# Chunked attention with routed MLP: 8-token load rows, PE transposes of halves, block-diagonal V, mask as bias, scatter-add output

## Chip, cores and metric

One core of one Trainium2 chip runs one launch. The metric is the device time of that launch in microseconds. The core has a matrix engine (TensorE, PE; its weight loads are listed apart as PEld), three elementwise engines (VectorE, DVE; ScalarE, ACT; GpSimd, POOL) and a queue engine (SyncE, SP). DMAs are issued here from the SP and POOL queues and run on 16 DMA engines. Every engine works through its own instructions in order.

## The reference

Attention runs in chunks of 32 queries; each chunk sees 8 memory slots and a window of keys from 16 before it to 8 after it. Then, for each of the 4 batch entries, the 128 of 768 tokens with the highest gate score get an MLP's output, times a sigmoid of the score, added.

```
q, k, v: (4, 8, 768, 64); mem_k, mem_v: (4, 8, 8, 64)
for each chunk c of 32:                       # 24 chunks
    k_full = concat(mem_k, k[c*32-16 : c*32+40]);  v_full the same   # clipped at the ends
    a = softmax(0.125 * q_c @ k_full.T);  out_c = a @ v_full
x = out as (4, 768, 512)
for b in range(4):
    s = x[b] @ w_gate;  top = the 128 largest of s
    y = relu(x[b, top] @ w1) @ w2             # 512 -> 1024 -> 512
    out[b, top] = x[b, top] + sigmoid(s[top]) * y
```

## The kernel before

A *group* is 96 queries (three chunks) of one head with 128 key rows: 8 memory slots and a window of 120 tokens. There are 8 groups to a head, 8 heads and 4 batches. The loop runs eight *phases* of (batch, half of the heads): four heads each.

- Set-up (lines 66 to 140). `identity` and the iotas come from POOL. The mask is three extra contraction rows in `qT` and `kT` (rows 64 to 66), filled by small DMAs from SP (L116, L125, L128), and zero blocks go into `v_sh` (L139, L140).
- A phase first issues its loads (L142): per head, q and k as fp32 from SP with 768 pieces of 256 bytes each (L148), V from POOL with a cast to fp16 (L164), and a POOL copy of the memory values (L166).
- Per head (L169): PE transposes of 128x128 fp32 (L175, L181), ACT copies qT out (L177, L178), DVE copies kT out twice and then lays the windows out (L183 to L192), and POOL adds the memory keys (L193).
- Per group (L196): four score matmuls (L200), one exponential of 384 columns on ACT (L203), four value matmuls with a ones column for the sum (L206), reciprocal and scaling on DVE (L209, L210) into `x_norm`, which stays in SBUF.
- The routed MLP of a batch: scores on DVE (L234), a row of scores by DMA and a POOL broadcast (L237, L239), rank by sign sums on ACT (L253), selection matrices on DVE (L257, L265), gather matmuls (L275), two MLP layers (L288, L298), then eight update matmuls (L307) and adds on DVE (L309) into `x_norm`, and one store of the whole batch (L313). MLP `b` is hooked into later phases: scoring and rank a batch later, the rest two batches later. After the last phase the MLP of batch 2 and all of batch 3 remain.
- A scheduler sets the order on each engine from the code's order and its own estimates; at run time the orders are fixed.

## Time and profile before

| | |
|---|---|
| time, median of 3 runs | 267.44 us (265.09 to 268.04) |
| span of the profiled execution | 263.0 us |
| set-up, to the first q tile used by PE | 0 to 30.9 us |
| first value matmul | 46.6 us |
| last scaled attention tile | 197.2 us |
| remaining MLP work and stores | 197.2 to 263.0 us |
| busy share PE, DVE, ACT, POOL | 57%, 61%, 46%, 27% |

The span is one execution; the time of a run holds some microseconds around it. Busy PE time counts the modelled latency of each matmul, so it overstates how full PE is. [...]

### The profile page before, as it was taken

Reading aid. Unit: us, or ns where it says so; the run is one execution under the profiler, and the core shown is the slowest. Engines: PE = TensorE matmul, PEld = TensorE weight load, DVE = VectorE, ACT = ScalarE, POOL = GpSimd, SP = SyncE. Lnnn points to the kernel's source line nnn. Section 1 sums busy time; section 2 is a strip of 40 time slices with the busy share of each in tenths; the row PEclk is TensorE's granted clock in tenths of the full one; section 3 lists DMA queues with packets and bytes.
Section 4 is the critical chain, followed back from the end, with each engine's and each line's share of the span. In section 5 each row is a group of like instructions: output and inputs, shape, how many; then the busy total and the mean of one; then the engine's idle time right before and its main releaser. Section 6 shows DMA issues by size and latency. Waiting matters only on the chain.

```text
span 263.0 us, 3436 instructions
## 1 busy us (share of the span) xinstructions
PE 151.1 (57%) x1056; PEld 110.3 (42%) x1056; DVE 159.9 (61%) x482; ACT 120.0 (46%) x260; POOL 70.9 (27%) x117
## 2 busy tenths in 40 slices
PE   0200255878867488658847778783682575487420
...
GB/s 50 32 181 116 117 157 157 220 190 142 202 168 35 172 135 179 147 145 67 30 98 98 240 22 58 0 0 94 148 0 0 2 2 0 1 237 3 0 47 192
DMA packets 90697, 25.55 MB, mean 97 GB/s; under 512 B 85944, under 2 KB 86968, under 8 KB 90680
## 3 DMA queue, kind: packets, MB, share of 16 engines
...
## 4 chain that ended last, share of the span: by engine, by line
PE 35%; DVE 26%; ACT 11%; DMA 8%; issue 8%; SPq 6%; POOL 3%; ACTq 0%; POOLq 0%
DVE xn L309 7%; PE p_upd L307 5%; PE pst L200 5%; PE pkt L181 5%; PE p_xeT L275 4%; PE pxv L206 4%; PE pqt L175 4%; DMA ksb<-in_k_dram 4%; DMA kT<-zeros_src 4%; PE p_hT L288 4%; SPq L148 3%; PE p_ye L298 3%; ACT expS L203 2%; DVE xn L210 2%; DVE kA L183 2%
## 5 line engine op out<-in xcount | busy, mean ns | idle before, releaser
L175 PE MATMUL pqt<-identity,qsb 128*128 128x128 f32 x96 | 28.0, 414 | 30.3 <-DMA qsb<-in_q_dram 24.2
L203 ACT ACTIVATE expS<-pst 128x384 f16<-128x384 f32 x64 | 30.4, 490 | 27.2 <-PE pst L200 26.0
L200 PE MATMUL pst<-qT,kT 67*128 67x96 f16 x256 | 37.3, 268 | 8.9 <-DVE kT L191 2.4
L177 ACT CAST qT<-pqt 64x384 f16<-64x384 f32 x32 | 15.1, 471 | 52.0 <-PE pqt L175 51.6
L181 PE MATMUL pkt<-identity,ksb 128*128 128x128 f32 x96 | 27.6, 406 | 11.9 <-ACT qT L178 4.9
L164 POOL DMA_DIRECT2D vsh<-in_v_dram x30 | 28.5, 951 | 19.8 <-PE pxv L206 19.8
L206 PE MATMUL pxv<-vsh,expS 128*96 128x65 f16 x256 | 31.0, 263 | 4.9 <-DVE rd L209 2.3
L206 PEld LDWEIGHTS <-expS 128*96 128x96 f16 x256 | 28.5, 189 | 12.2 <-ACT expS L203 5.6
L175 PEld LDWEIGHTS pqt<-identity,qsb 128*128 128x128 f32 x96 | 16.0, 206 | 40.8 <-DMA qsb<-in_q_dram 19.7
L200 PEld LDWEIGHTS <-kT 67*128 67x128 f16 x256 | 25.2, 135 | 18.9 <-issue 9.7
L309 DVE TENSOR_TENSOR xn<-p_upd,xn 96x512 f32<-96x512 f32 x32 | 21.9, 683 | 18.4 <-PE p_upd L307 18.2
L183 DVE CAST kA<-pkt 64x384 f16<-64x384 f32 x32 | 17.5, 546 | 22.8 <-PE pkt L181 22.6
L253 ACT ACTIVATE junk_rk<-Bsb,scores 96x768 f32<-96x768 f32 x32 | 29.8, 932 | 0.6
L210 DVE TENSOR_TENSOR xn<-pxv,rd 96x256 f32<-96x256 f32 x64 | 26.5, 414 | 0.8
L307 PE MATMUL p_upd<-ye,selT 128*96 128x512 f16 x32 | 16.7, 522 | 16.9 <-DVE xn L309 15.1
L275 PE MATMUL p_xeT<-sel,x 96*128 96x128 f16 x128 | 18.1, 305 | 14.1 <-DVE sel L257 13.3
L166 POOL COPY vsh<-memv_all 8x512 f16<-8x512 f16 x32 | 21.7, 690 | 10.9 <-DMA memv_all<-in_mem_v_dram 10.9
L193 POOL COPY kT<-memkT_sb 64x64 f16<-64x64 f16 x32 | 6.9, 256 | 60.8 <-PE pst L200 60.8
L181 PEld LDWEIGHTS pkt<-identity,ksb 128*128 128x128 f32 x96 | 15.3, 200 | 17.0 <-ACT qT L178 7.3
L234 DVE SCALAR_TENSOR_TENSOR junk_sc<-xn,wgb 96x512 f32<-96x512 f32 x32 | 21.7, 677 | 0.2
L209 DVE RECIPROCAL rd<-pxv 96x4 f32<-96x4 f32 x64 | 11.2, 175 | 15.8 <-PE pxv L206 15.1
L275 PEld LDWEIGHTS <-x 96*128 96x128 f16 x128 | 14.3, 143 | 14.4 <-issue 13.9
...
## 6 DMA issues: line engine op xcount, KB each, us to landing
...
vsh<-in_v_dram POOLq DMA_DIRECT2D x30, 120.0 KB, 7.9
w_sb<-in_moe_w_dram POOLq DMA_DIRECT2D x2, 1024.0 KB, 11.0
...
vsh<-in_v_dram POOLq DMA_DIRECT2D x2, 105.0 KB, 4.7
qT<-ones_src SPq DMA_DIRECT2D x12, 0.5 KB
```

The source lines that it names most:

```text
L164: nc.gpsimd.dma_start(out=v_sh[8:128, h, :, 0:D], in_=_dap(v, base - 16 * D, [[D, 120], [96 * D, 8], [1, D]]))
L175: nc.tensor.transpose(out=pq[:, pr, :], in_=q_sb[:, h4, pr, :], identity=identity)
L181: nc.tensor.transpose(out=pk[:, pr, :], in_=k_sb[:, h4, pr, :], identity=identity)
L183: nc.vector.tensor_copy(out=kae[:, :, 0, :], in_=pk[0:64, :, :])
L200: nc.tensor.matmul(out=p_st[:, h4, :], lhsT=kT_ext[h4][0:67, g, :], rhs=qT_ext[h4][0:67, GQ * g:GQ * g + GQ], start=True, stop=True)
L203: nc.scalar.activation(out=es, in_=p_st[:, :, :], func=AF.Exp, bias=0.0, scale=0.125)
L206: nc.tensor.matmul(out=p_x[0:GQ, h4, :], lhsT=es[:, h4, :], rhs=v_sh[:, h4, g, :], start=True, stop=True)
L210: nc.vector.tensor_tensor(out=x_norm[0:GQ, g, :].rearrange("p (h d) -> p h d", d=D)[:, NH * hq:NH * hq + NH, :], in0=p_x[0:GQ, :, 0:D], in ...
L253: nc.scalar.activation(out=m.junk_rk[0:GQ, :], in_=m.Bsb[0:GQ, :], func=AF.Sign, bias=m.scores[0:GQ, g:g + 1], scale=-1.0, accum_out=m.cod ...
L275: nc.tensor.matmul(out=m.p_xeT[:, dch, :], lhsT=m.x16[0:GQ, g, 128 * dch:128 * dch + 128], rhs=m.sel16[0:GQ, g, :], start=(g == 0), stop=( ...
L307: nc.tensor.matmul(out=m.p_upd[0:GQ, g % 2, :], lhsT=m.selT[:, g, :], rhs=m.ye, start=True, stop=True)
L309: nc.vector.tensor_tensor(out=x[0:GQ, g, :], in0=m.p_upd[0:GQ, g % 2, :], in1=x[0:GQ, g, :], op=ALU.add)
```

## The change

Nearly the whole kernel function is rewritten.

- **Loads.** q and k are loaded by POOL with a cast to fp16, as rows of 8 tokens (512 elements, 2 KB of DRAM) on 96 partitions: 4 DMAs a batch after the first. V stays fp32 and comes from SP in rows of two tokens (512 bytes), head 0 of a pair on partitions 0 to 63 and head 1 on 64 to 127, 60 rows of window and 4 of memory.
- **Units.** The work is cut into 16 pairs of heads with 2 halves each (32 units of 4 groups). For a pair, 16 PE transposes of a 96x64 fp16 piece for q and 16 for k (`tr_q`, `tr_k`) put token slot j of 8 into one PSUM tile; ACT lays q out with one copy of 768 columns, DVE k with three copies. POOL casts V into `vbd`, where the two heads lie block-diagonally with a ones column each, one slice for even and one for odd tokens.
- **Scores and values.** 16 score matmuls a unit (64 keys of one head, one parity, 96 queries), three exponentials on ACT with the mask as bias per partition, and 12 value matmuls of 130 columns: 6 with 96 queries and 6 with 32, so that a unit fills 128 partitions of `x`.
- **MLP.** The batch is stored as soon as its attention is done (`m_store`). The row of scores comes by PE transposes, the rank by six compares of 768 columns with a sum on DVE, the slot by a matmul. The result is gated on DVE and added into the output rows in DRAM by an indirect DMA (`m_ffn2`). The update matmuls, the adds in SBUF and the two row DMAs are gone. MLP `b` runs one batch later, a step a unit; only batch 3's remains behind the last unit.
- PSUM: one buffer for transposes (`ptt`), one for the MLP (`pmm`), two each for scores and values.

The diff, cut to the new functions that matter (what is removed stands in the kernel above):

```diff
+    def load_qk(b, src, dst, p0, n):
+        h0 = 2 * p0
+        nc.gpsimd.dma_start(out=dst[:, h0:h0 + 2 * n, :],
+                            in_=_dap(src, (b * H + h0) * HD, [[512, 96], [HD, 2 * n], [1, 512]]))
...
+            o = 64 * h
+            for i in range(n):
+                nc.sync.dma_start(out=t[o:o + 60, p0 + i, 1:7, :],
+                                  in_=_dap(v, base + 2 * i * HD + 80 * D, [[2 * D, 60], [96 * D, 6], [1, 128]]))
...
+            for i in range(n):
+                nc.sync.dma_start(out=t[o + 60:o + 64, p0 + i, :, :],
+                                  in_=_dap(mem_v, (b * H + 2 * (p0 + i) + h) * n_mem * D,
+                                           [[2 * D, 4], [0, NG], [1, 128]]))
...
+    memk16 = cst.tile([n_mem, B * H, D], F16, tag="memk16")
+    nc.gpsimd.dma_start(out=memk16, in_=_dap(mem_k, 0, [[D, n_mem], [n_mem * D, B * H], [1, D]]))
+    alloc_batch(0)
+    load_qk(0, q, q16s[0], 0, 1)
+    load_qk(0, k, k16s[0], 0, 1)
+
+    ident = cst.tile([128, 128], FP, tag="ident")
+    make_identity(nc, ident)
...
+    load_v(0, 0, 1)
+    load_qk(0, q, q16s[0], 1, 1)
+    load_qk(0, k, k16s[0], 1, 1)
...
+        nc.gpsimd.memset(vb[0:64, :, :, 65:130], 0.0)
+        nc.gpsimd.memset(vb[64:128, :, :, 0:65], 0.0)
...
+    def tr_q(n):
+        b, pr = divmod(n, NP)
+        p_t = ptt.tile([128, 8, 96], F16, tag="tp", name="p_tq")
+        for j in range(8):
+            for h in range(2):
+                nc.tensor.transpose(out=p_t[64 * h:64 * h + 64, j, :],
+                                    in_=q16s[b][:, 2 * pr + h, 64 * j:64 * j + 64],
+                                    identity=ident16[0:96, 0:96])
+        qT = att.tile([128, 96, 8], F16, tag="qT", name="qT")
+        nc.scalar.copy(out=qT, in_=p_t.rearrange("p j t -> p t j"))
...
+        p_t = ptt.tile([128, 8, 96], F16, tag="tp", name="p_tk")
+        for j in range(8):
+            for h in range(2):
+                nc.tensor.transpose(out=p_t[64 * h:64 * h + 64, j, :],
+                                    in_=k16s[b][:, 2 * pr + h, 64 * j:64 * j + 64],
+                                    identity=ident16[0:96, 0:96])
+        kw = kws[n % SLOTS]
+        nc.vector.tensor_copy(out=kw[:, 1:7, 0:120].rearrange("p g (t j) -> p g t j", j=8),
+                              in_=_sap(p_t, 10, [[12, 6], [1, 15], [96, 8]]))
...
+        nc.gpsimd.tensor_copy(out=kw[:, :, 120:128], in_=memkT[:, n:n + 1, :].to_broadcast([128, NG, n_mem]))
...
+        for h in range(2):
+            o = 64 * h
+            nc.gpsimd.tensor_copy(out=vb[o:o + 64, :, :, 65 * h:65 * h + 64],
+                                  in_=v32s[b][o:o + 64, pr, :, :].rearrange("p g (s d) -> p g s d", d=D))
...
+    GROUPS = ((0, 1, 2, 6), (3, 4, 5, 7))
...
+        for gi, g in enumerate(GROUPS[half]):
+            for s in range(2):
+                for h in range(2):
+                    o = 64 * h
+                    nc.tensor.matmul(out=p_s[o:o + 64, s, 96 * gi:96 * gi + 96],
+                                     lhsT=kw[o:o + 64, g, s:128:2],
+                                     rhs=qf[o:o + 64, 96 * g:96 * g + 96], start=True, stop=True)
+        es = att.tile([128, 2, 4, 96], F16, tag="es", name="es")
+        pv = p_s[:, :, 0:384].rearrange("p s (g t) -> p s g t", t=96)
+        for c in range(3):
+            nc.scalar.activation(out=es[:, :, :, 32 * c:32 * c + 32], in_=pv[:, :, :, 32 * c:32 * c + 32],
+                                 func=AF.Exp, bias=maskb[:, c:c + 1], scale=0.125)
...
+        p_x = pxx.tile([128, 3, 130], FP, tag="px", name="p_x")
+        for gi in range(3):
+            for s in range(2):
+                nc.tensor.matmul(out=p_x[0:96, gi, :], lhsT=es[:, s, gi, :], rhs=vb[:, GROUPS[half][gi], s, :],
+                                 start=(s == 0), stop=(s == 1))
+        for c in range(3):
+            for s in range(2):
+                nc.tensor.matmul(out=p_x[96:128, c, :], lhsT=es[:, s, 3, 32 * c:32 * c + 32],
+                                 rhs=vb[:, GROUPS[half][3], s, :], start=(s == 0), stop=(s == 1))
+        pv = p_x.rearrange("p g (h d) -> p g h d", d=65)
+        rd = att.tile([128, 3, 2, 1], FP, tag="rd", name="rd")
+        nc.vector.reciprocal(out=rd, in_=pv[:, :, :, 64:65])
+        nc.vector.tensor_tensor(
+            out=xs[b][:, 3 * half:3 * half + 3, 128 * pr:128 * pr + 128].rearrange("p g (h d) -> p g h d", d=D),
+            in0=pv[:, :, :, 0:64], in1=rd.to_broadcast([128, 3, 2, D]), op=ALU.mult)
...
+    def m_store(b):
+        x = xs[b]
+        nc.sync.dma_start(out=_dap(out, b * S * Dm, [[Dm, 96], [96 * Dm, NB], [1, Dm]]), in_=x[0:96, :, :])
+        nc.sync.dma_start(out=_dap(out, (b * S + 576) * Dm, [[Dm, 32], [32 * Dm, NB], [1, Dm]]), in_=x[96:128, :, :])
...
+        for bl in range(lo, hi):
+            junk = mod.tile([128, Dm], FP, tag="junk", name="junk")
+            nc.vector.scalar_tensor_tensor(out=junk, in0=x[:, bl, :], scalar=1.0, in1=wgb,
+                                           op0=ALU.mult, op1=ALU.mult, accum_out=m.scr[:, bl:bl + 1])
+        nc.gpsimd.tensor_copy(out=m.x16[:, lo:hi, :], in_=x[:, lo:hi, :])
...
+        for lo, hi in ((0, 4), (4, 6)):
+            p_b = pmm.tile([128, 4, 128], FP, tag="pm", name="p_b")
+            for bl in range(lo, hi):
+                nc.tensor.transpose(out=p_b[:, bl - lo, :], in_=m.scr[:, bl:bl + 1].to_broadcast([128, 128]),
+                                    identity=ident)
+            nc.scalar.copy(out=m.brow[:, 128 * lo:128 * hi].rearrange("p (c t) -> p c t", t=128),
+                           in_=p_b[:, 0:hi - lo, :])
...
+            nc.vector.tensor_scalar(out=jr, in0=m.brow, scalar1=m.scr[:, bl:bl + 1], scalar2=None,
+                                    op0=ALU.is_gt, op1=ALU.add, accum_out=m.cnt[:, bl:bl + 1])
...
+        nc.vector.tensor_tensor_scan(out=incl, data0=ones6, data1=mask, initial=0.0, op0=ALU.mult, op1=ALU.add)
+        p_p = pmm.tile([128, 1], FP, tag="pm", name="p_p")
+        nc.tensor.matmul(out=p_p, lhsT=ltri, rhs=incl[:, NB - 1:NB], start=True, stop=True)
...
+        for bl in range(NB):
+            nc.vector.tensor_scalar(out=m.sel[:, bl, :], in0=iota1, scalar1=slot[:, bl:bl + 1], scalar2=None,
+                                    op0=ALU.is_equal)
...
+        for dch in range(4):
+            for bl in range(NB):
+                nc.tensor.matmul(out=p_e[:, dch, :], lhsT=m.x16[:, bl, 128 * dch:128 * dch + 128],
+                                 rhs=m.sel[:, bl, :], start=(bl == 0), stop=(bl == NB - 1))
+        m.xeT = mod.tile([128, 4, 128], F16, tag="xeT", name="xeT")
+        nc.scalar.copy(out=m.xeT, in_=p_e)
...
+        for bl in range(NB):
+            nc.tensor.matmul(out=p_a, lhsT=m.sel[:, bl, :], rhs=auxs[b % 2][:, bl, :],
+                             start=(bl == 0), stop=(bl == NB - 1))
+        m.idx = mod.tile([128, 1], I32, tag="idx", name="idx")
+        nc.vector.tensor_scalar(out=m.idx, in0=p_a[:, 0:1], scalar1=float(b * S), scalar2=None, op0=ALU.add)
...
+        m = mods[b]
...
+        nc.vector.tensor_scalar(out=y, in0=p_y, scalar1=m.gate[:, 0:1], scalar2=None, op0=ALU.mult)
+        nc.gpsimd.indirect_dma_start(out=outf, out_offset=bass.IndirectOffsetOnAxis(ap=m.idx[:, :1], axis=0),
+                                     in_=y[:, :], in_offset=None, compute_op=ALU.add)
...
+    def moe_steps(b):
+        return [
+            [lambda: m_store(b), lambda: m_scores(b, 0, 3)],
+            [lambda: m_scores(b, 3, 6), lambda: m_rows(b)],
+            [lambda: m_rank(b, 0, 3)],
+            [lambda: m_rank(b, 3, 6), lambda: m_select(b)],
+            [lambda: m_gather(b)],
+            [lambda: m_ffn1(b, 0)],
+            [lambda: m_ffn1(b, 1)],
+            [lambda: m_ffn2(b)],
+        ]
...
+    tr_q(0)
+    tr_k(0)
+    cast_v(0)
+    scores(0)
+    tr_q(1)
+    for u in range(NU):
+        n, half = divmod(u, 2)
+        b, bu = divmod(u, 8)
+        if u + 1 < NU:
+            scores(u + 1)
+        if half == 0 and n + 1 < NPR:
+            tr_k(n + 1)
+            cast_v(n + 1)
+        if half == 1 and n + 2 < NPR:
+            tr_q(n + 2)
+        if bu == 1 and b + 1 < B:
+            load_batch(b + 1)
+        if u == 2:
+            load_w()
+        values(u)
+        if b >= 1:
+            for f in moe_steps(b - 1)[bu]:
+                f()
```

On POOL at the start of the program, before (identity, the iotas and the first loads):

```order
masks.py:197 MEMSET identity 128x128
L70 ISA
L70 IOTA iota_row 128x128
masks.py:199 AFFINE_SELECT identity<-identity 128x128
L73 IOTA iota_col 128x1
L84 DMA w_sb<-in_moe_w_dram 128x4x1024
L86 DMA w_sb<-in_moe_w_dram 128x8x512
L91 DMA memv_all<-in_mem_v_dram 8x32x64
L156 DMA vsh_215<-in_v_dram 104x64
```

and now (`q_0`, `k_0` are batch 0's q and k; `ident` is the identity):

```order
L99 DMA memk_84<-in_mem_k_dram 8x32x64
L77 DMA q_0_86<-in_q_dram 96x2x512
L77 DMA k_0_87<-in_k_dram 96x2x512
masks.py:197 MEMSET ident 128x128
L77 DMA q_0_86<-in_q_dram 96x2x512
masks.py:199 ISA
masks.py:199 AFFINE_SELECT ident<-ident 128x128
L77 DMA k_0_87<-in_k_dram 96x2x512
L77 DMA q_0_86<-in_q_dram 96x4x512
L77 DMA k_0_87<-in_k_dram 96x4x512
L132 IOTA kp 64x1 x2
L160 MEMSET vbd_158 64x16x65
```

Four loads now stand ahead of the instruction that makes the identity, and the clearing of `vbd` (eight such MEMSETs in all), some iotas and then the casts of V follow behind the loads.

On PE, in the middle of the program before (a value matmul and its weights, then score matmuls of two heads):

```order
L206 LDWEIGHTS expS
L206 MATMUL pxv<-vsh_221,expS 96x65
L200 LDWEIGHTS kT_150
L200 MATMUL pst<-qT_149,kT_150 128x96
L200 LDWEIGHTS kT_166
L200 MATMUL pst<-qT_165,kT_166 128x96
```

and now in batch 0 (the last value matmuls of the first unit, with 32 queries, then score matmuls):

```order
L270 LDWEIGHTS es
L270 MATMUL p_x<-vbd_158,es 32x130
L270 LDWEIGHTS es
L270 MATMUL p_x<-vbd_158,es 32x130
L245 LDWEIGHTS kw_167
L245 MATMUL p_s<-qT,kw_167 64x96
L245 LDWEIGHTS kw_167
L245 MATMUL p_s<-qT,kw_167 64x96
```

Each matmul now fills fewer rows of the array's output (32, 64 or 96 where it was 96 or 128), the score matmuls alternate between partitions 0 to 63 and 64 to 127, and there are more of them.

On DVE at the end of the program, before (selection for batch 3, then its eight adds):

```order
L257 TENSOR_SCALAR sel_2337<-i_row,code 96x128
L309 TENSOR_TENSOR xn_227<-p_upd,xn_227 96x512
L257 TENSOR_SCALAR sel_2337<-i_row,code 96x128
L309 TENSOR_TENSOR xn_227<-p_upd,xn_227 96x512
L257 TENSOR_SCALAR sel_2337<-i_row,code 96x128 x5
L265 SCALAR_TENSOR_TENSOR selT<-Bcode,i_col,Bsig 128x96 x8
L309 TENSOR_TENSOR xn_228<-p_upd,xn_228 96x512 x8
```

and now (rank, selection, indices and the gated result of batch 3):

```order
L325 TENSOR_SCALAR jr,cnt<-brow,scr 128x768
L318 TENSOR_TENSOR aux_219<-gt,aux_219 128x6
L325 TENSOR_SCALAR jr,cnt<-brow,scr 128x768 x5
L331 TENSOR_SCALAR mask<-cnt 128x6
L333 SCALAR_TENSOR_TENSOR incl<-ones_214,mask 128x6
L337 SCALAR_TENSOR_TENSOR slot<-incl,p_p,mask 128x6
L340 TENSOR_SCALAR sel<-iota_209,slot 128x128 x6
L357 TENSOR_SCALAR idx<-p_a 128x1
L359 TENSOR_REDUCE gate<-p_a 128x1
L378 TENSOR_SCALAR y<-p_y,gate 128x512
```

The sixteen adds and their selection matrices are gone from the end, and the rank has moved there from ACT.

## Rows read from the trace of the kernel before

**Rows 1.** Windows: us busy (instructions) of PE, PEld, DVE, ACT, POOL; granted clock; DMA; GB/s

```profile
0.00:30.90 30.90, 1.87 (x32) 1.78 (x32) 7.07 (x30) 1.79 (x3) 11.47 (x27) 1.00 0.57 95
...
46.60:197.20 150.60, 109.38 (x829) 84.97 (x830) 119.53 (x367) 88.72 (x188) 50.94 (x82) 0.61 0.94 112
197.20:263.00 65.80, 31.09 (x160) 18.01 (x159) 26.65 (x66) 25.20 (x61) 3.15 (x3) 0.55 0.16 48
```

**Rows 2.** The page: busy time, share of the span and instructions of each engine

```profile
PE 151.1 (57%) x1056; PEld 110.3 (42%) x1056; DVE 159.9 (61%) x482; ACT 120.0 (46%) x260; POOL 70.9 (27%) x117
```

**Rows 3.** Timeline at the start: start, duration (us), engine, line, operation [idle before]

```profile
1.94 2.12 SPq L116 DMA_DIRECT2D qT<-ones_src  x3
...
8.89 0.24 POOL L70 IOTA iota_row<- 128x128 f32 x1 [7.96 <-issue]
...
28.06 0.44 SPq L148 DMA_DIRECT2D qsb<-in_q_dram  x1
...
30.94 0.90 PE L175 MATMUL pqt<-identity,qsb 128*128 128x128 f32 x3 [19.62 <-DMA qsb<-in_q_dram]
...
46.60 0.53 PE L206 MATMUL pxv<-vsh,expS 128*96 128x65 f16 x4 [0.48 <-ACT expS L203]
```

**Rows 4.** Timeline of PE while the granted clock was 0.5

```profile
190.89 0.53 PE L206 MATMUL pxv<-vsh,expS 128*96 128x65 f16 x4 [0.46 <-ACT expS L203]
...
206.39 2.83 PE L275 MATMUL p_xeT<-sel,x 96*128 96x128 f16 x25 [0.79 <-DVE sel L257]
...
215.56 3.57 PE L298 MATMUL p_ye<-w_sb,hT 128*128 128x512 f16 x8 [0.87 <-ACT hT L291]
```

**Rows 5.** Timeline of PE while the granted clock was 1.0

```profile
161.31 0.50 PE L175 MATMUL pqt<-identity,qsb 128*128 128x128 f32 x3
...
162.78 1.05 PE L288 MATMUL p_hT<-xeT,w_sb 128*128 128x128 f16 x16 [0.55 <-ACT hT L291]
...
168.69 0.37 PE L206 MATMUL pxv<-vsh,expS 128*96 128x65 f16 x4
```

**Rows 6.** Groups by line and shape, DVE: count, total us, mean ns, idle before

```profile
L210 DVE TENSOR_TENSOR xn<-pxv,rd 96x256 f32<-96x256 f32 x64 | 26.5, 414 | 0.8
...
L309 DVE TENSOR_TENSOR xn<-p_upd,xn 96x512 f32<-96x512 f32 x32 | 21.9, 683 | 18.4 <-PE p_upd L307 18.2
...
L234 DVE SCALAR_TENSOR_TENSOR junk_sc<-xn,wgb 96x512 f32<-96x512 f32 x32 | 21.7, 677 | 0.2
...
L183 DVE CAST kA<-pkt 64x384 f16<-64x384 f32 x32 | 17.5, 546 | 22.8 <-PE pkt L181 22.6
...
L209 DVE RECIPROCAL rd<-pxv 96x4 f32<-96x4 f32 x64 | 11.2, 175 | 15.8 <-PE pxv L206 15.1
```

**Rows 7.** Timeline of POOL at the start

```profile
0.72 0.20 POOL masks.py:197 MEMSET identity<- 128x128 f32 x1 [0.29 <-POOLq L383]
...
12.72 0.77 POOL L193 COPY kT<-memkT_sb 64x64 f16<-64x64 f16 x4
...
24.41 4.51 POOL L166 COPY vsh<-memv_all 8x512 f16<-8x512 f16 x8 [10.92 <-DMA memv_all<-in_mem_v_dram]
```

**Rows 8.** Groups by line and shape, POOL: the loads of V

```profile
L164 POOL DMA_DIRECT2D vsh<-in_v_dram x30 | 28.5, 951 | 19.8 <-PE pxv L206 19.8
```

**Rows 9.** Timeline at the end

```profile
196.82 0.42 DVE L210 TENSOR_TENSOR xn<-pxv,rd 96x256 f32<-96x256 f32 x1
...
230.06 3.80 PE L275 MATMUL p_xeT<-sel,x 96*128 96x128 f16 x32 [0.78 <-DVE xn L309]
...
243.51 0.59 ACT L300 CAST ye<-p_ye 128x512 f16<-128x512 f32 x1 [3.36 <-PE p_ye L298]
...
254.60 0.32 SPq L313 DMA_DIRECT2D out_dram<-xn  x1
```

**Rows 10.** DMA issues: count, KB each, median us to landing

```profile
w_sb<-in_moe_w_dram POOLq DMA_DIRECT2D x2, 1024.0 KB, 11.0
...
vsh<-in_v_dram POOLq DMA_DIRECT2D x2, 105.0 KB, 4.7
```

More of the change, by code (lines that the diff above doesn't have):

```diff
@@ L217, with load_w @@
-    x_norms = [xpool.tile([128, NG, Dm], FP, tag=f"xn{b % 3}", name=f"xn{b}") for b in range(B)]
+    def load_w():
+        nc.gpsimd.dma_start(out=w1_sb, in_=_dap(moe_w1, 0, [[F, 128], [128 * F, 4], [1, F]]))
+        nc.gpsimd.dma_start(out=w2_sb, in_=_dap(moe_w2, 0, [[Dm, 128], [128 * Dm, 8], [1, Dm]]))
+    kp = cst.tile([128, 1], FP, tag="kp")
+    for h in range(2):
+        nc.gpsimd.iota(kp[64 * h:64 * h + 64, :], pattern=[[0, 1]], base=0, channel_multiplier=1,
+                       allow_small_or_imprecise_dtypes=True)
@@ new lines @@
+    p_mk = ptt.tile([128, B * NP, n_mem], F16, tag="tp", name="p_mk")
+    for pr in range(B * NP):
+        nc.tensor.transpose(out=p_mk[:, pr, :], in_=memk16[:, 2 * pr:2 * pr + 2, :],
+                            identity=ident16[0:n_mem, 0:n_mem])
+    memkT = cst.tile([128, B * NP, n_mem], F16, tag="memkT")
+    nc.vector.tensor_copy(out=memkT, in_=p_mk)
+    iota1 = cst.tile([128, cap], F16, tag="iota1")
+    nc.gpsimd.iota(iota1, pattern=[[1, cap]], base=1, channel_multiplier=0, allow_small_or_imprecise_dtypes=True)
@@ L269, in mod_ffn_a @@
-    def mod_ffn_a(b):
-        m = mods[b]
-        m.xeT = mod.tile([128, 4, 128], F16, tag="xeT", name="xeT")
-        m.p_xeT = pm.tile([128, 4, 128], FP, tag="pm", name="p_xeT")
-        for dch in range(4):
-            for g in range(NG):
-                nc.tensor.matmul(out=m.p_xeT[:, dch, :], lhsT=m.x16[0:GQ, g, 128 * dch:128 * dch + 128],
-                                 rhs=m.sel16[0:GQ, g, :], start=(g == 0), stop=(g == NG - 1))
-        for dch in range(4):
-            nc.scalar.copy(out=m.xeT[:, dch, :], in_=m.p_xeT[:, dch, :])
@@ new lines, in m_ffn1, with m_ffn2 @@
+    def m_ffn1(b, half):
+        m = mods[b]
+        p_h = pmm.tile([128, 4, 128], FP, tag="pm", name="p_h")
+        for fi in range(4):
+            f0 = 128 * (4 * half + fi)
+            for dch in range(4):
+                nc.tensor.matmul(out=p_h[:, fi, :], lhsT=w1_sb[:, dch, f0:f0 + 128], rhs=m.xeT[:, dch, :],
+                                 start=(dch == 0), stop=(dch == 3))
+        nc.scalar.activation(out=m.hT[:, 4 * half:4 * half + 4, :], in_=p_h, func=AF.Relu)
+    def m_ffn2(b):
```

415 lines of the change are left out of this document (149 added, 266 removed).

## The prediction

> **What bounds the kernel now.** I read the windows first. They cut the span into a start in which almost nothing computes (PE busy 1.87 of 30.9 us), a middle of 150.6 us in which the attention runs and which holds the MLPs of batches 0 and 1, and an end of 65.8 us with the rest of the MLPs [rows 1]. The page's shares alone (PE 57%, DVE 61%) name no engine [rows 2]; in the middle DVE is busy 119.5 of 150.6 us (79%) and PE 109.4, at a mean granted clock of 0.61 [rows 1].
>
> The timeline explains the start. SP spends its first 27 us issuing the small mask DMAs, three of them in 2.12 us, and turns to q only at 28.06; PE takes its first q tile at 30.94 and the first value matmul comes at 46.60 [rows 3]. POOL stands still for 7.96 us before its first iota [rows 3]; the order shows its ISA instruction just there, so I read the gap as the price of that instruction.
>
> The end is a serial chain: after the last scaled tile at 196.82 the gather of batch 3 starts only at 230.06, and the last store leaves at 254.60 [rows 9], followed by 8 us until the span ends.
>
> So I price three stages: until the first value matmul, the units, and the chain behind the last unit. The sum is made against the span of 263.0 us. The median of the runs is 267.4, so 4.4 us are added at the end.
>
> **Start.** The mask DMAs are gone; POOL's queue is now what the first unit waits for. It starts at 0.72 [rows 7]. Four loads at 0.95 us each [rows 8] are 3.8, the MEMSET 0.2 [rows 7], the ISA 8.0 [rows 3], the identity's select 0.3: 13.0 us, when PE can begin to transpose (30.9 before). Then three loads (2.9) and two iotas (0.3) give 16.2. A POOL copy of 64 columns took 0.77/4 = 0.19 us and one of 512 took 4.51/8 = 0.56 [rows 7], so 0.83 ns a column and 0.14 fixed. Eight clears of 1040 columns are then 1.0 each, or half that if two fp16 go at once; I take 1.0, since the MEMSET of 128 columns lies on the same line (0.20). That is 24.2; six small set-up instructions take about 1, and the memory keys and two casts of 1024 columns 2.3. **First value matmul at 27.5 us** (23.5 with cheap clears), 19 earlier than before.
>
> **The units.** PE's prices at half clock: 25 matmuls of 128 columns in 2.83 us are 0.105 each, 0.82 ns a column; 512 columns take 3.57/8 = 0.446; four value matmuls take 0.53 although their 65 columns follow weights of 96, so weights load beside the matmul before and whichever is longer sets the pace [rows 4]. At full clock 16 of 128 columns take 1.05 and the four take 0.37 [rows 5], so the fixed part does not halve.
>
> A pair of heads has 32 transposes and 32 score matmuls, each of 96 columns, and 24 value matmuls of 130 columns. Before, no matmul used a quarter or half of the array beside another one, so the price of the 64 small ones has to be bounded. Above it is 0.079 us (96 columns, one after the other). Below it is 0.053 (neighbours in the other half stream together and the weights of 64 columns set the pace). I take the middle, 0.066, as no row is nearer to either end. With 0.107 for 130 columns a pair costs 64 x 0.066 + 24 x 0.107 = 6.8 us (6.0 to 7.6) at half clock.
>
> [...]
>
> The MLP adds to each of the last three batches: 24 gather and 32 first-layer matmuls at 0.105 (5.9), 8 of 512 columns (3.6), 6 fp32 transposes at 0.30 (0.90 for three [rows 3]; 1.8), a few small ones (0.4): 11.7. A batch is 4 x 6.8 + 11.7 = 38.9 us at half clock. At the middle's mean clock of 0.61 [rows 1] it is 31.9. To that come waits on single PSUM buffers: between `tr_q` and `tr_k` PE stands until ACT's copy of 768 columns is out (0.59 for 512 [rows 9], so 0.85, and 0.25 of latency), 4 x 1.1 = 4.4; the MLP's five hand-overs of 0.6, a third of them uncovered by other PE work, 2. **38.3 us a batch**, 115 for three.
>
> Batch 0 has no MLP. Up to its last value matmul the order lists 352 transposes and score matmuls (those of the next batch's first pairs among them) and 96 value matmuls: 34.5 us at half clock, of which 9.4 lie ahead of 27.5. The rest, 25 us, gives its end at 52.5. I leave the half clock there: three fp32 transposes take 0.90 at 30.94 [rows 3] and 0.50 at full clock [rows 5], so the start runs at half although its window is listed at 1.00 [rows 1].
>
> What the other engines do lies beside this. DVE: 256 columns from PSUM take 0.414 and 512 take 0.683 [rows 6], about 0.145 fixed and 1.05 ns a column. A pair then takes 1.4 for the three k copies (720, 104, 112 columns; the 384-column cast at 0.546 agrees), 0.35 for two reciprocals and 1.1 for two scalings: 2.9. The MLP takes 6 scorings at 0.70 with their reads, 6 ranks of 768 columns at 0.95, and 3.3 for the rest: 13. That is 24.6 a batch, under 38. POOL: eight casts of 1.0, four memory-key copies, two fp16 copies of x at 1.4, four loads, the scatter: 16 to 17. ACT: six exponentials of 256 columns and one copy of 768 a pair, under 3.2 a pair with the MLP. Loads: the same bytes, but 25,000 pieces of 512 bytes to 2 KB replace 80,000 of 256; 1 MB of fp16 weights landed in 11.0 us [rows 10], so a batch's loads fit well into 38 us. If that cover went, q of the next batch would hold PE's in-order queue, at some 10 us a batch.
>
> **The end.** Behind the last unit: five scorings 3.6; transposes and ACT copies of the score row 1.5; six ranks 6.3; mask, scan, matmul, slot and six selections 2.0. From gather to the second layer's result took 244.1 - 230.06 = 14.0 us before [rows 9]. Eight gather matmuls fewer save 0.9 and single evacuations 0.6; the index matmuls through the one bank add 1.2; the gating replaces the cast: 13.7. The scatter is unknown here: issue as a load, 0.95 [rows 8], landing between 2 us and the 11.0 of the large load; I take 4.7, a load of 105 KB [rows 10], and 0.7 to end. **33.5 us**, where 65.8 stood [rows 1].
>
> Sum: 27.5 + 25 + 115 + 33.5 = 201 us of span, 205.5 as a time: **206 us**.
>
> **Rivals.** *DVE sets the pace (176 us).* If neighbours stream together and PE's density lifts its clock, a batch is PE 4 x 6.0 + 11.7 = 36 at half and 18 at full clock, so DVE's 24.6 rules; at its present 79% that is 31 a batch. 27.5 + 20 + 93 + 31.5 + 4.4 = 176. For it: full clock occurs in dense stretches [rows 5]. Against it: in the middle the mean was 0.61 with PE busy 73% [rows 1]. Chance 0.24.
>
> *Changes of tile shape empty the array (226 us).* A unit goes from half-array to quarter-array to full-array to a 32-column strip, about 8 changes a pair. If each exposes a matmul's latency (the last of four adds about 0.26, less the 0.08 it would have cost [rows 4]: 0.18), 16 pairs cost 23 us, of which some 20 show: 206 + 20. Nothing before changes shape this often, so no row decides. [...] Chance 0.18.
>
> *No overlap, half clock throughout (242 us).* A pair is 7.6, a batch 42.1 + 6.4 = 48.5; batch 0 ends at 57: 57 + 145.5 + 35 + 4.4. Chance 0.08.
>
> *Slower than before (317 us).* If the small matmuls' weights do not load beside the previous matmul, each of 1024 costs 0.053 + 0.079 = 0.132, and the 384 value matmuls their 96 or 32 columns more: 55 and 20 us on top of 242. From about 0.104 us for a small matmul on the time reaches 267. Against it: the value matmuls of [rows 4] hide weights of 96 columns. Chance 0.06.
>
> **How the numbers follow.** The forecast itself has 0.42; 0.02 is left for anything else, no change included. The range takes in the rivals from 176 to 242 and the cheap clears: 172 to 245. A change within 1% can't be told from none in this measurement. The first four cases are faster; the cases near 267 are split: faster 0.91, within 1% 0.03, slower 0.06.
>
> **What would show it.** First value matmul at 25 to 30 us, with the ISA gap and the MEMSETs ahead of it on POOL; 16 transposes in about 1.3 us; units of batches 1 to 3 at 4 to 5.5 us with PE as the engine others wait for; 30 to 36 us behind the last scaled tile. Wrong would be: 16 score matmuls in over 2 us; a middle where PE waits mostly for casts, q or DVE; a scatter of over 8 us.

## The result and the profile after

The changed kernel takes **200.4 us** (median of four runs, 199.3 to 204.6) where the kernel before takes 266.3 beside it: ratio 0.755, 95% interval 0.748 to 0.763. Forecast were 206 us and a range of 172 to 245. The profiled execution took 200.0 us, 198.6 of them span. One of the four runs came out over 1.5% above the fastest (204.6), as some runs of other kernels here do; kernels are compared without such runs where that decides.

The windows, cut at the last scaled tile of each batch (as in [rows 1]: length, busy time of PE, weight loads, DVE, ACT and POOL, granted clock as a share of full speed, DMA share, GB/s):

```profile
0.00:51.70 51.70, 28.80 (x501) 23.56 (x502) 23.19 (x76) 18.17 (x38) 35.74 (x57) 0.87 1.00 187
51.70:86.30 34.60, 28.01 (x364) 20.72 (x362) 25.29 (x66) 13.43 (x31) 14.24 (x19) 0.70 0.99 199
86.30:127.00 40.70, 31.12 (x462) 23.69 (x461) 26.98 (x65) 16.35 (x37) 14.66 (x15) 0.75 0.43 97
127.00:167.90 40.90, 26.60 (x334) 19.99 (x334) 28.27 (x67) 11.74 (x27) 13.55 (x11) 0.71 0.18 46
167.90:198.60 30.70, 10.69 (x76) 6.81 (x76) 13.24 (x39) 2.94 (x6) 5.24 (x3) 0.64 0.30 69
```

No engine is busy all the time in any of them, though together they leave little free: in batch 3 PE works 26.6 and DVE 28.3 of 40.9 us. In the first two rows the 16 DMA engines are full (1.00, 0.99); later they are mostly idle.

PE's row in time (start, duration, engine, line, operation, weights' rows*columns) shows the start, which answers [rows 3], and the prices, which answer [rows 4, 5]:

```profile
17.05 0.85 PE L201 MATMUL p_tq<-ident,q 96*64 96x96 f16 x16 [6.61 <-DVE kw L221]
...
21.87 1.49 PE L245 MATMUL p_s<-qT,kw 64*64 64x96 f16 x32
23.28 0.85 PE L213 MATMUL p_tk<-ident,k 96*64 96x96 f16 x16
24.07 0.88 PE L266 MATMUL p_x<-vbd,es 128*96 128x130 f16 x6
24.88 0.83 PE L270 MATMUL p_x<-vbd,es 128*32 128x130 f16 x6
25.64 0.84 PE L245 MATMUL p_s<-qT,kw 64*64 64x96 f16 x16
26.42 0.55 PE L266 MATMUL p_x<-vbd,es 128*96 128x130 f16 x6
```

The last of the first six value matmuls by itself, the same place in a later unit, and a change from the second MLP layer to values, the last two at full clock (granted 1.00 from 118.9 to 124 us):

```profile
24.64 0.32 PE L266 MATMUL p_x<-vbd,es 128*96 128x130 f16 x1
```
```profile
118.97 0.53 PE L245 MATMUL p_s<-qT,kw 64*64 64x96 f16 x16
119.42 0.53 PE L201 MATMUL p_tq<-ident,q 96*64 96x96 f16 x16
...
121.33 0.22 PE L266 MATMUL p_x<-vbd,es 128*96 128x130 f16 x1
121.48 0.23 PE L270 MATMUL p_x<-vbd,es 128*32 128x130 f16 x1
...
121.94 0.82 PE L376 MATMUL p_y<-w_sb,hT 128*128 128x512 f16 x3
122.59 0.51 PE L266 MATMUL p_x<-vbd,es 128*96 128x130 f16 x6
```

The profile has no record of the clock before 26.4 us and lists 1.00 there; the prices say half clock, since 16 transposes hold PE for the same 0.79 us at 61.38, where the granted clock is recorded as 0.50.

Sixteen transposes hold PE for 24.07 - 23.28 = 0.79 us (0.049 on average) at half clock and 0.45 (0.028) at full clock; six value matmuls for 0.81 and 0.76 (0.135 and 0.127 on average), at full clock 0.46 (0.077). These averages mix two things. Thirty-two scores take 23.28 - 21.87 = 1.41 us and sixteen 26.42 - 25.64 = 0.78, so sixteen more cost 0.63, 0.039 each, and each group holds some 0.15 us beside that. The single matmuls show where it lies: inside a group, small matmuls start in pairs 0.080 us apart (0.043 at full clock) and value matmuls 0.107 to 0.111 apart (0.055 to 0.061) once the first two are past. Where the tile shape changes, the next start comes later: 0.21 us after a small matmul and 24.88 - 24.64 = 0.24 after a value matmul at half clock, 0.13 and 0.15 at full. A change so costs 0.13 to 0.14 us at half clock and about 0.09 at full. From 128x512 matmuls to 96-column values nothing is added: three of them take 122.59 - 121.94 = 0.65 us, 0.22 each, which is their own price.

POOL's queue, against [rows 7, 8]:

```profile
4.54 0.33 POOL masks.py:199 TENSOR_SCALAR_AFFINE_SELECT ident<-ident 128x128 f32<-128x128 f32 x1
...
7.22 0.96 POOL L160 MEMSET vbd<- 64x1040 f16 x1
...
16.70 1.03 POOL L230 CAST vbd<-v 64x1024 f16<-64x1024 f32 x1
...
28.33 2.16 POOL L230 CAST vbd<-v 64x1024 f16<-64x1024 f32 x2
...
31.60 1.03 POOL L230 CAST vbd<-v 64x1024 f16<-64x1024 f32 x1 [0.81 <-DMA v<-in_mem_v_dram]
...
42.65 1.06 POOL L230 CAST vbd<-v 64x1024 f16<-64x1024 f32 x1 [10.01 <-DMA v<-in_mem_v_dram]
```

A batch has eight such casts. Batch 0's begin at 16.70, 18.04, 19.35 (two), 24.35 (two) and 28.33 (two) and are done at 30.5 us. The waits of 0.81 and 10.01 us are for V of batch 1's first pair.

DVE's copies of ones beside the clears, the first by itself and then all eight:

```profile
12.30 0.99 DVE L164 COPY vbd<-ones 64x16 f16<-64x16 f16 x1
```
```profile
12.30 4.32 DVE L164 COPY vbd<-ones 64x16 f16<-64x16 f16 x8
```

The group of scorings on the page (busy us, mean ns of one), where [rows 6] had 677 ns for one:

```profile
L298 DVE SCALAR_TENSOR_TENSOR junk<-x,wgb 128x512 f32<-128x512 f32 x24 | 30.6, 1301 | 0.1
```

The scorings are the surprise, and DVE's row with POOL's shows what becomes of them one by one, DVE first:

```profile
82.57 0.69 DVE L298 SCALAR_TENSOR_TENSOR junk<-x,wgb 128x512 f32<-128x512 f32 x1
...
83.19 1.94 DVE L298 SCALAR_TENSOR_TENSOR junk<-x,wgb 128x512 f32<-128x512 f32 x1
...
128.75 0.67 DVE L298 SCALAR_TENSOR_TENSOR junk<-x,wgb 128x512 f32<-128x512 f32 x1
...
129.36 3.52 DVE L298 SCALAR_TENSOR_TENSOR junk<-x,wgb 128x512 f32<-128x512 f32 x1
```
```profile
82.60 1.99 POOL L300 CAST x<-x 128x1536 f16<-128x1536 f32 x1 [2.54 <-DVE x L275]
...
129.75 2.58 POOL L230 CAST vbd<-v 64x1024 f16<-64x1024 f32 x2
```

The scoring that began at 129.36 took 3.52 us and ended at 132.88, 0.55 us behind the two casts that POOL ran from 129.75 to 132.33. The one at 82.57 began before POOL's copy of x and took 0.69; the one at 83.19 began within that copy, took 1.94 and ended 0.54 us behind it. So it goes throughout: twelve of the 24 scorings take 0.64 to 0.69 us, and the other twelve, 0.91 to 3.52 us long, each end 0.54 to 0.56 us behind a copy or cast of POOL.

Last, SP's queue and the end, which answers [rows 9]:

```profile
SPq L288 <- DMA out_dram<-y,idx: 73.2, 3, 40.3
```
```profile
93.81 0.33 SPq L288 DMA_DIRECT2D out_dram<-x  x1
...
94.79 3.74 SPq L86 DMA_DIRECT2D v<-in_v_dram  x2
...
174.82 0.32 SPq L288 DMA_DIRECT2D out_dram<-x  x1
```
```profile
191.31 0.75 DVE L378 TENSOR_SCALAR y<-p_y,gate 128x512 f32<-128x512 f32 x1 [6.72 <-PE p_y L376]
192.34 1.55 POOL L379 DMA_INDIRECT out_dram<-y,idx  x1 [20.51 <-DVE y L378]
```

The wait of 40.3 us is that of the last store, of batch 3, behind which no load stands. The store at 93.81, ahead of batch 3's V, had waited 10.8 us.

The last scaled tile starts at 167.37 and the scatter at 192.34; the span ends 4.7 us after its issue of 1.55 us.

### The profile page after: what moved, and what is told of

It is laid out like the page before. It is cut to its first block, busy times and chain, and to the rows that moved or that the text cites. A ratio compares the mean times of both kernels' runs of the same rounds, so it can differ in the third digit from the quotient of the medians.

```text
span 198.6 us, 4328 instructions
## 1 busy us (share of the span) xinstructions
PE 125.2 (63%) x1732; PEld 94.8 (48%) x1732; DVE 117.0 (59%) x309; ACT 62.6 (32%) x137; POOL 83.4 (42%) x104
## 5 line engine op out<-in xcount | busy, mean ns | idle before, releaser
L251 ACT ACTIVATE es<-p_s,maskb 128x256 f16<-128x256 f32 x96 | 37.8, 476 | 34.2 <-PE p_s L245 31.1
L230 POOL CAST vbd<-v 64x1024 f16<-64x1024 f32 x32 | 35.5, 1158 | 12.8 <-DMA v<-in_mem_v_dram 10.8
L298 DVE SCALAR_TENSOR_TENSOR junk<-x,wgb 128x512 f32<-128x512 f32 x24 | 30.6, 1301 | 0.1
L245 PE MATMUL p_s<-qT,kw 64*64 64x96 f16 x512 | 23.9, 247 | 4.5 <-DVE kw L219 2.5
L245 PEld LDWEIGHTS <-kw 64*64 64x64 f16 x512 | 18.3, 137 | 12.5 <-issue 4.7
L325 DVE TENSOR_SCALAR_CACHE_REDUCE jr<-brow,scr 128x768 f16<-128x768 f32 x24 | 23.0, 1001 | 1.2 <-ACT brow L310 1.2
L266 PE MATMUL p_x<-vbd,es 128*96 128x130 f16 x192 | 21.2, 259 | 2.3 <-ACT es L251 0.9
L270 PE MATMUL p_x<-vbd,es 128*32 128x130 f16 x192 | 19.9, 248 | 0.0
L266 PEld LDWEIGHTS <-es 128*96 128x96 f16 x192 | 16.4, 149 | 6.1 <-ACT es L251 2.4
L275 DVE TENSOR_TENSOR x<-p_x,rd 128x384 f32<-128x384 f32 x32 | 17.5, 551 | 0.6
L348 PE MATMUL p_e<-sel,x 128*128 128x128 f16 x96 | 13.3, 304 | 1.9 <-DVE sel L340 1.9
## 6 DMA issues: line engine op xcount, KB each, us to landing
w_sb<-in_moe_w_dram POOLq DMA_DIRECT2D x2, 1024.0 KB, 20.6
```

What stands on the lines that cost most here:

```text
L230: nc.gpsimd.tensor_copy(out=vb[o:o + 64, :, :, 65 * h:65 * h + 64], in_=v32s[b][o:o + 64, pr, :, :].rearrange("p g (s d) -> p g s d", d=D))
L245: nc.tensor.matmul(out=p_s[o:o + 64, s, 96 * gi:96 * gi + 96], lhsT=kw[o:o + 64, g, s:128:2], rhs=qf[o:o + 64, 96 * g:96 * g + 96], start= ...
L251: nc.scalar.activation(out=es[:, :, :, 32 * c:32 * c + 32], in_=pv[:, :, :, 32 * c:32 * c + 32], func=AF.Exp, bias=maskb[:, c:c + 1], scal ...
L266: nc.tensor.matmul(out=p_x[0:96, gi, :], lhsT=es[:, s, gi, :], rhs=vb[:, GROUPS[half][gi], s, :], start=(s == 0), stop=(s == 1))
L270: nc.tensor.matmul(out=p_x[96:128, c, :], lhsT=es[:, s, 3, 32 * c:32 * c + 32], rhs=vb[:, GROUPS[half][3], s, :], start=(s == 0), stop=(s ...
L275: nc.vector.tensor_tensor(out=xs[b][:, 3 * half:3 * half + 3, 128 * pr:128 * pr + 128].rearrange("p g (h d) -> p g h d", d=D), in0=pv[:, : ...
```

## Experiments

All times are medians of four runs (six in run 10) beside the kernel before on the same chip, unless said otherwise; the changed kernel's 200.4 us is the reference. A scheduler sets each engine's order from its own estimates, so an edit also reorders instructions elsewhere; where that decides, it is said.

**1. The scorings without POOL's copies of x.**

```
-        nc.gpsimd.tensor_copy(out=m.x16[:, lo:hi, :], in_=x[:, lo:hi, :])
+        nc.scalar.copy(out=m.x16[:, lo:hi, :], in_=x[:, lo:hi, :])
```

> The fp16 copies of x (two of 128x1536 per batch) go from POOL to ACT; nothing else in the source. Theory 1: DVE's scorings are slow because POOL copies beside them; with the V casts still on POOL the mean scoring falls from 1.30 to about 0.9 us, DVE's busy time by about 10 us, and the time from 200 to about 194 us (192 to 198), since the MLP chain of the batch before sets the pace of batches 2 and 3. Rival: the scorings are slow for another reason (the time from the changed kernel's own data or its DMAs); then they stay at 1.2 to 1.3 us and the time at 200 +- 2. Second rival: DVE is relieved, but PE's order hides it; scorings 0.9, time 200 +- 2.

Measured 187.4 us (186.6 to 188.2; ratio to before 0.706, 0.700 to 0.712).

**2. The V casts on ACT too** (both edits):

```
-            nc.gpsimd.tensor_copy(out=vb[o:o + 64, :, :, 65 * h:65 * h + 64],
+            nc.scalar.copy(out=vb[o:o + 64, :, :, 65 * h:65 * h + 64],
```

> The V casts (32 of 64x1024) go to ACT as well, so that POOL keeps only its DMA issues, small copies and the clears. Theory 1: scorings at 0.70 us throughout, POOL busy from 83 to about 35 us, ACT from 63 to about 110, time about 190 us (186 to 196). Rival: ACT now has exponentials queued behind casts, PE waits for es instead of DVE, and the time is 200 us or more although the scorings are at 0.70.

Measured 195.4 us (193.0 to 197.5; 193.5 without the two slowest). The group of scorings on the page of the first and of the second run, and what PE's value matmuls waited for in the second:

```profile
L298 DVE SCALAR_TENSOR_TENSOR junk<-x,wgb 128x512 f32<-128x512 f32 x24 | 20.0, 867 | 0.1
```
```profile
L298 DVE SCALAR_TENSOR_TENSOR junk<-x,wgb 128x512 f32<-128x512 f32 x24 | 15.6, 678 | 0.1
```
```profile
L266 PE MATMUL p_x<-vbd,es 128*96 128x130 f16 x192 | 21.5, 260 | 9.4 <-ACT vbd L230 4.8 <-ACT es L251 4.3 <-DVE x L275 0.4
```

The mean goes 1301, 867, 678 ns as POOL is emptied in two steps, so POOL's copies and casts beside it are what slows a scoring. The first edit is worth 13 us. The scorings got 10.6 us shorter by it, but it also takes the x copies out of POOL's queue ahead of V's casts, and the granted clock of batches 1 and 2 rose from 0.70 and 0.75 to 0.82 and 0.85; how the 13 us divide is not shown. The second step gives the scorings all back and yet costs about 6 us against the first: PE now waits 9.4 us ahead of line 266, for ACT's casts (4.8) and its exponentials (4.3), where it waited 2.8. That is the rival's wait, though the time stayed inside the theory's range and below the rival's 200. The loss lies in batch 1, 35.8 instead of 28.5 us, where DVE's order and the arrival of V changed too, so it is not shown to be ACT's alone.

**3. One head, then the other.** In `scores`, `tr_q` and `tr_k` the loop over the two heads becomes the outer one:

```
-            for s in range(2):
-                for h in range(2):
+        for h in range(2):
+            for gi, g in enumerate(GROUPS[half]):
+                for s in range(2):
```

> Scores and transposes of a pair are issued all of one head and then all of the other, so that neighbours no longer lie in different halves of the array. Theory 1: the 0.040 us pitch of the small matmuls is two neighbours in different halves running side by side; now 16 of them take about 1.3 us at half clock instead of 0.85 and 0.65 to 0.7 at full clock instead of 0.53, PE's busy time goes from 125 to 145 to 160 us, and the time to 208 to 218 us. Rival: the pitch is that of any 64x64 matmul of 96 columns, whatever its neighbour: nothing moves, 200 +- 2 us. Second rival: PE is slower but has the slack in the waits for DVE: pitch 0.08, time under 205.

Measured 214.9 us (213.9 to 215.4; ratio 0.810, 0.803 to 0.817). PE's row at half and at full clock, and its busy time:

```profile
102.95 1.18 PE L245 MATMUL p_s<-qT,kw 64*64 64x96 f16 x16
104.06 1.18 PE L213 MATMUL p_tk<-ident,k 96*64 96x96 f16 x16
...
131.38 0.73 PE L245 MATMUL p_s<-qT,kw 64*64 64x96 f16 x16
132.04 0.73 PE L201 MATMUL p_tq<-ident,q 96*64 96x96 f16 x16
```
```profile
PE 147.5 (69%) x1732; PEld 116.2 (54%) x1732; DVE 114.7 (54%) x309; ACT 62.7 (29%) x137; POOL 83.2 (39%) x104
```

Sixteen now hold PE for 1.11 us at half clock (0.069 on average) and 0.66 at full (0.041), against 0.79 and 0.45: neighbours in different halves do overlap. Neighbours in one half start 0.080 us apart at half clock and 0.042 at full, where a pair of different halves did before. PE is busy 22 us more (125.2 before this edit), at a slightly lower mean clock (0.72 instead of 0.75), and the time grows by 14.6: some two thirds of PE's extra work shows although PE also waits for DVE.

**4. Clearing slots 2 and 3 behind the first unit** (`init_slot(i)` holds lines 154 to 165; slots 0 and 1 stay in front):

```
         values(u)
+        if u == 0:
+            init_slot(2)
+            init_slot(3)
```

> Slots 2 and 3 are cleared behind the first unit's values instead of ahead of everything (four of eight POOL MEMSETs and four of eight DVE copies of ones move). Theory: the clears and their copies held the first unit; the first value matmul comes at 19 to 20 us instead of 24.1, but batch 0 still ends at 51 to 52 us since its V loads set that; time 200 +- 1.5 us. Rival: the whole gain of 4 to 5 us is kept, 195 to 196 us.

The first value matmul comes at 16.0 us instead of 24.1, earlier than the theory's 19 to 20, and batch 0's last tile starts at 49.0 instead of 51.1. The median is 199.0, the runs lie between 196.1 and 204.0; the two quicker ones, 196.1 and 196.5, lie some 4 us under the changed kernel's 199.3 to 200.7. So about 4 of 8 us of start are left, near the rival's figure.

**5. V ahead of the store.** From batch 2 on `load_batch` runs at a batch's first unit, and `xp` has three buffers:

```
-        if bu == 1 and b + 1 < B:
+        if bu == (1 if b == 0 else 0) and b + 1 < B:
```

> From batch 2 on the loads of a batch are issued one unit earlier, so that its V loads stand ahead of the store of x on SP's queue (in the changed kernel that store waits for the scatter of the MLP before, and 16 V loads of batch 3 wait behind it until 94.8 us), and x has three buffers instead of two. Theory: the units of batch 3 come late because their V loads and x buffer hang on that chain; now half of them run ahead of the second gather, the last scaled tile comes at 156 to 161 us instead of 167.9, and the time is 190 us (186 to 195). Rival: the serial MLP chain on DVE alone sets the pace; the units move but the last scaled tile stays within 2 us, time 198 to 202 us.

Measured 194.1 us (193.3 to 196.3; ratio 0.736, 0.729 to 0.743), the last tile at 156.4. What SP did, and a wait that is new:

```profile
77.13 0.34 SPq L288 DMA_DIRECT2D out_dram<-x  x1
...
79.04 4.31 SPq L86 DMA_DIRECT2D v<-in_v_dram  x2
```
```profile
POOL out_dram L379 <- DMA out_dram<-x: 22.2, 2, 11.2
```

V of batch 3 is issued at 79 instead of 95 us, but the store of batch 0 has gone from 51.7 to 77.1 behind V of batch 2, and scatters now wait for stores, 22.2 us in two waits. The gain is 11.0 us at the last tile (156.4 instead of 167.4) and 6 in the time: the end takes 34.9 us instead of 31.2, at a granted clock of 0.57 instead of 0.65, and its scatter was held by a store for 1.6 us.

The number holds; the cause that the theory gives is not shown. In the changed kernel V of batch 3 was cast by 140.7, long before its first values stand in PE's order, at 153.48 behind the gather and first layer of batch 2's MLP, which wait for the ranks on DVE (138.5 to 144.2). In this run they come at 138 to 141, ahead of that gather. The third buffer of `xp` was not tested apart from the order of the loads.

**6. Other loads behind V of batch 0** (batch 1's at unit 3 instead of 1, the weights at unit 8 instead of 2):

```
-        if bu == 1 and b + 1 < B:
+        if bu == (3 if b == 0 else 1) and b + 1 < B:
             load_batch(b + 1)
-        if u == 2:
+        if u == 8:
             load_w()
```

> The loads of batch 1 are issued at unit 3 instead of 1 and the weights at unit 8 instead of 2. Theory: batch 0's end at 51.6 us was set by its V loads, which shared the DMA engines with both; POOL's wait of 10 us for V goes, batch 0 ends at 40 to 45 us, and the time falls to 190 to 196 us. Rival: the DMA engines are full in either order until 86 us, so batch 1's loads come that much later, batch 1 ends at 84 to 88 us as before, and the time stays at 198 to 202 us.

Measured 191.9 us (189.7 to 192.7; ratio 0.726, 0.719 to 0.732). Batch 0's last tile comes at 43.2 and batch 1's at 77.2 (51.1 and 85.7 before this edit): the times are the theory's, and the gain is 8.5 us in the median. Its mechanism is not what the trace shows. V of batch 0 was cast by 30.5 us in both kernels, and POOL still waits for V of batch 1 (2.59 us at 35.87, 8.35 at 57.22). What differs is PE's order: the scores of batch 0's last two units, here and in the changed kernel,

```profile
35.95 0.87 PE L245 MATMUL p_s<-qT,kw 64*64 64x96 f16 x32
```
```profile
43.90 1.49 PE L245 MATMUL p_s<-qT,kw 64*64 64x96 f16 x32
```

stood in the changed kernel behind transposes for batch 1, which waited for ACT's and DVE's copies of the transposed q and k. So the place of those loads in the program is worth some 8 us, by what they change in the orders; how much of it is their place in the DMA queues is open.

**7. One broadcast on POOL** (one run):

```
     make_identity(nc, ident)
+    nc.gpsimd.partition_broadcast(pbx, ident[0:1, 0:8], channels=128)
```

> One partition broadcast of 128x8 is added on POOL behind the identity; its result is not used. In the kernel before, POOL stood still for 7.96 us ahead of its first iota, and the prediction took that for the price of the ISA instruction which stands there. Theory: such a gap belongs to a change between two sets of POOL instructions, which the broadcasts of the kernel before bring in; here one or two gaps of 7 to 9 us appear at the broadcast and behind it, POOL's first V cast comes 8 to 17 us later, the first value matmul at 32 to 41 us. Rival: no gap, the first value matmul stays at 24 to 25 us.

POOL's row:

```profile
4.82 0.33 POOL masks.py:199 TENSOR_SCALAR_AFFINE_SELECT ident<-ident 128x128 f32<-128x128 f32 x1 [0.33 <-issue]
...
14.40 0.28 POOL L107 PARTITION_BROADCAST pbx<-ident  x1 [8.63 <-issue]
...
28.45 0.33 POOL L134 IOTA kp<- 64x1 f32 x2 [12.34 <-issue]
```

It stands still for 8.63 us ahead of the broadcast and 12.34 us ahead of the iota behind it; at the identity, where the prediction had put 8 us, it stands 0.33. Both gaps stand where the theory put them, the second longer than its 7 to 9 us. What POOL did in them the trace does not show, and no run shows whether the 7.96 us in [rows 3] are of the same kind. The first tile is scaled at 42.7 instead of 26.1 us, and the time is 201.4 us: 17 us of late start cost 1, in a single run and at a mean clock of 0.81 instead of 0.75. The order differs here as well (some of batch 3's units precede the MLP of batch 2), so the run shows that the start did not decide the end, not by which work it was swallowed.

**8. Edits 1, 4 and 5 together.**

> Three edits at once: x's fp16 copies on ACT, slots 2 and 3 cleared late, V loads ahead of the store with three x buffers. Alone the first gave 13 us and the second 1; the third is run beside this. Theory: DVE's scorings and the order of units and MLP are two limits of which each hides a part of the other: 180 us (175 to 186). Rival: one of the two alone is the limit, and the time stays at that of the first edit, 186 to 189 us.

Measured 180.0 us (177.6 to 181.8): the theory's number. Alone the three edits gained 13.0, 1.4 and 6.2 us in the medians, 20.6 in all, and together 20.4: they add up, where the theory had each limit hide a part of the other. Its number came, its reason did not.

**9. Edit 6 on top.**

> The three edits of the combined kernel (180.0 us) and the later loads of batch 1 and of the weights, which alone took 8 us off the changed kernel. Theory: in the combined kernel batch 0 still ends at 50.8 us because of its V loads, so these 8 us are another limit; the time falls to 172 us (168 to 176). Rival: the chain of MLPs and scatters absorbs the earlier end of batch 0, as it absorbed the earlier start; 178 to 182 us.

Measured 176.5 us (173.9 to 177.9; ratio 0.671, 0.663 to 0.679). Batch 0 ends 8.9 us earlier than in run 8 (last tile 41.3 instead of 50.2), of which 3.5 are left in the median, between theory and rival.

**10. Three of the last six ranks on ACT:**

```
+            if b == B - 1 and bl >= 3:
+                nc.scalar.activation(out=ja, in_=m.brow, func=AF.Sign, bias=m.scr[:, bl:bl + 1], scale=-1.0,
+                                     accum_out=m.cnt[:, bl:bl + 1])
```

> As the kernel with all edits, and in the last MLP three of the six ranks go to ACT (Sign with a sum) beside DVE's three. Theory: the end is a serial chain in which six ranks of 0.94 us stand on DVE while ACT is idle; it gets 2.5 us shorter (1.5 to 3), and the time with it, 169 to 170 us if the kernel with all edits takes 172. Rival: the chain moves to ACT's ranks or to the transposed row; under 1 us.

Measured 174.0 us (170.3 to 176.0; ratio 0.648, 0.639 to 0.658), 2.5 below run 9 in the median, as expected, though the runs of the two overlap. In the profiles the ranks take 2.9 instead of 5.7 us and the stretch from the last tile's start to the end 28.8 instead of 30.3. It is the fastest version here, 13% below the changed kernel.

**11. The kernel before without its mask DMAs:**

```
-        for j in range(3):
-            nc.sync.dma_start(out=kt[64 + j:65 + j, :, 8 + 32 * j:64 + 32 * j],
-                              in_=zeros_src[0:1, 0:8 * 56])
...
```

> The kernel before, without its 32 small mask and edge DMAs on SP: the mask rows are zero (the mask is left out) and the edges of V are zeroed by DVE. SP turns to q at 2 to 4 us instead of 28. Theory, the prediction's sum of stages: the first value matmul comes about 20 us earlier, DVE at 79% sets the middle's pace as before, and the time falls by as much: 246 us (242 to 251). Rival: a late start is swallowed later, as the run with the broadcast swallowed 17 us in the changed kernel; 258 to 267 us.

Measured 257.1 us (256.1 to 257.3; ratio 0.974, 0.964 to 0.984). The first value matmul comes 13.3 us earlier, the last tile 8.6:

```profile
33.27 0.34 PE L195 MATMUL pxv<-vsh,expS 128*96 128x65 f16 x2
```
```profile
27.48 1.16 POOL L155 COPY vsh<-memv_all 8x512 f16<-8x512 f16 x2 [11.74 <-DMA memv_all<-in_mem_v_dram]
```

The next wait was queued right behind: POOL stood 11.74 us for the memory values, whose DMA came behind the weights. Both sides missed: the expectation had SP as the start's only limit; of the 13.3 us, 8.6 are left at the last tile and 7.4 in the time.

## Why the prediction held, and where its steps failed

The time lay 6 us below the forecast. By stages (in us):

| Stage | predicted | measured |
|---|---|---|
| first value matmul | 27.5 | 24.1 |
| rest of batch 0 | 25 | 27.6 |
| batches 1, 2, 3 | 38.3 each, 115 | 34.6, 40.7, 40.9: 116.2 |
| behind the last tile | 33.5 | 30.7 |
| span | 201 | 198.6 |
| time less span | 4.4 | 1.4 |

The sizes are close; the reasons behind them are right in part only, and errors of both signs met.

**Time less span.** Of the 6 us, 3 are this term. The 4.4 came from the median of some runs and the span of another execution; within one and the same run time and span lie 1.7 to 2.3 us apart in all runs on record, before and after.

**Start.** The clears cost 0.96 to 0.98 us each as priced (1.0), and one term fell: the 8.0 us for the ISA instruction were 0 here (in run 7, 0.33 at the identity, with 8.63 and 12.34 around the broadcast). So POOL's second cast ended at 19.1, where 27.5 was forecast. The other 5 us came back by a wait that the sum did not have: `tr_q(1)` at 17.05 waited 6.61 us for the k copies, since DVE spent 4.32 us on eight copies of ones. The first three took 0.99 to 1.00 us each and each ended 0.06 us behind a clear of POOL; the last four, with the clears over, took 0.20 each. The pattern is like that of the slow scorings, which ended 0.54 to 0.56 us behind a copy or cast of POOL. Run 4 took half of the clears away and the start fell to 16.0.

**Small matmuls and changes of tile shape.** Taken was 0.066 us, bounds 0.053 and 0.079. Within a group they measured 0.040: a pair of neighbours takes what one was priced at, so the lower bound was too high. Run 3 shows the cause to be overlap of neighbours in different halves. The 0.107 for 130 columns held. Left out was what the rival of 226 us had priced, the change of tile shape: 0.13 to 0.14 us at half clock and about 0.09 at full, where the rival took 0.18, and 8 a pair as it counted. Between 128x512 and 96-column matmuls the rows show no step: 0.22 us to the next start, as between two of 128x512 (full clock). A pair so takes 64 x 0.040 + 24 x 0.108 + 8 x 0.135 = 6.2 us, and 6.3 by the groups above, where 6.8 stood: 1.7 too much for the small ones and 1.1 too little for the changes, which met by luck. The added time at a change was there, about three quarters of what the rival took for it (that the array empties is not shown); the rival's total was not, since the overlap more than paid for it.

**Clock.** 0.61 was carried over from the middle of before; it was 0.70 to 0.75 in batches 1 to 3. PE's 31.9 us a batch became 28.0, 31.1 and 26.6. The kernel before shows other values too: beside runs 5 to 8, it took 263.1 us at a mean clock of 0.79 and 263.9 at 0.68. To carry one value over was a guess.

**What paced the batches.** Here the step failed that let PE and its hand-overs set the pace (31.9 + 6.4). PE idles 6.6, 9.6 and 14.3 us in the three. One cause is the term "scorings at 0.70": they take 1.30, so 24 of them hold DVE for 14 us more than priced; run 1, which mends a part of that, gives back 13. In batch 3 the way is seen in PE's row: no value matmul runs from 127 to 153.5 us, since in PE's order they stand behind the gather and first layer of batch 2's MLP, which wait for the ranks that DVE begins at 138.5, behind the slow scorings. The kernel before gave no warning: its 32 scorings took 0.66 to 0.76 us each. Here the scoring at 82.57, begun 0.03 us before POOL's copy, took 0.69, the one at 83.19, begun within that copy, 1.94; the one at 129.36 began by its record 0.39 us before POOL's casts and yet took 3.52; twelve of the 24 end 0.54 to 0.56 us behind a copy or cast of POOL. By what means POOL holds them no run shows. The other cause lies with the loads, which "fit well into 38 us": in bytes they do, and POOL waits for V at two places only. But moving them gives 8 us (run 6) and 6 (run 5). Both edits change the engines' orders as well, and neither trace shows V's arrival as what PE had waited for, so this cause is open. "Wrong would be a middle where PE waits mostly for casts, q or DVE": for DVE, it did, at the predicted time.

**The end.** Scatter and rest came as summed, 0.95 + 4.7 + 0.7 = 6.35 predicted and 198.6 - 192.34 = 6.3 measured, by two misses that met: the issue took 1.55, and the rest 4.7 instead of 5.4. The ranks took 5.7 against 6.3.

**Sum of stages.** Adding the stages took each for a chain of its own. Runs 4, 7 and 11 speak against it: starts moved by -8, +17 (one run) and -13 us changed the time by about -4, +1 and -7.4. The rival at 176 us (DVE sets the pace) named the wrong single engine, but runs 8 to 10 reach its time once the slow scorings, the clears and the order of the loads are mended.
